# Converting the second chunk of w_out in two halves in a fused FFT and two-layer FFN kernel

## The chip, the cores and the metric

The kernel runs on one core of a Trainium2 chip. The metric is the device time of one execution in microseconds (us). The engines are PE (matrix multiplies, with its weight loads shown apart as PEld), DVE (vector), ACT (scalar), POOL (GpSimd) and SP, which here only issues DMAs. Each engine works through its own instructions in the order in which the program gives them.

## The reference, cut to what matters

```
X = fft(fft(x, axis=1), axis=2).real        # x: 2 x 3008 x 256
h = X @ w_in;  g = where(h > 0, h, exp(min(h, 0)) - 1)
y = g @ w_out                               # w_in 256 x 2048, w_out 2048 x 256
h2 = y @ w2_in; out = (max(h2, 0) + alpha * min(h2, 0)) @ w2_out
```

x and alpha are float32. The four weight matrices come as 64-bit numbers. The kernel has to make 32-bit floats of them itself, on the chip, before it can multiply with them.

## The kernel before, in words

**Stages.** The program builds the Fourier transform out of matrix products (stage_a, a store to DRAM and a load in another order, stage_b), folds the last transform into w_in (w_fold), and runs the first layer as 96 "ticks". A tick t takes one slice f of 128 hidden units over one block of tokens. The first eight ticks are block 0 with f = 0 to 7, the next eight block 1 with f = 0 to 7. The second layer comes after the ticks, in 48 "pairs".

**A tick** (lines 593 to 647) issues, in this order: the "pre" hooks; gemm1(t) on PE (six matmuls, L472); on DVE one pt (L605) and two ht (L609) out of the two PSUM banks; on ACT split_hi of tick t-2 (L584); the "mid" hooks; on ACT Relu (L625) and Exp (L631) of tick t; on POOL split_lo of tick t-2 (two subtractions, L590); on DVE combine of tick t-1 (L577); the "end" hooks; and last on PE gemm2 of tick t-3 (twelve matmuls, L488). Where a tick is the eighth of its block, gemm2 and the copies of its banks (evac, L506 and L508) come earlier in the tick. gemm2 of slice f multiplies with rows 128 f to 128 f + 127 of w_out: slices 0 to 3 need chunk 0, slices 4 to 7 chunk 1. So the first half of chunk 1 is first needed at the end of tick 7, its second half at the end of tick 9, and the second half of chunk 0 at the end of tick 5. Each multiplication is done in three passes with a high and a low part of each operand, and for those slices the second matmul already needs the low part of the weight.

**Converting a chunk.** A chunk of a weight matrix is loaded raw (line 320, an int32 tile of 128 x 4 x 512 for w_out, 8 KB in each partition). conv_y (line 333, ACT) and three steps of conv_s (lines 351, 353 and 355, DVE) make a float32 copy w32 of 128 x 1024 out of it; the steps 0 and 1 work inside the raw tile, and step 2 is the last to read it. Then w_split makes the high part (line 430, ACT) and the low part (line 431, POOL) of one half of 512 columns, in a tile wo of 128 x 2 x 4 x 256, also 8 KB: the high parts are in its first 4 KB, the low parts in its last 4 KB, each with the first half ahead of the second. An argument i restricts conv_y and conv_s to one half of the columns: half i is the raw tile's 4 KB from 4 KB x i on.

**Where the tiles lie.** The pool wp has one buffer for each tag. The raw tile of chunk 1 and its wo tile have the same tag, wo1, so they lie in the same 8 KB. The raw tile of chunk 0 is an exception (line 216): it lies in the buffer of wo3, into which chunk 3 is loaded at the start of tick 4 (line 828). The first w_split of a chunk (i = 0) takes the new tile out of the pool (line 413); no engine waits by hand, the waits come from the order in which tiles are used.

**What sets the order around the change.** Lists written out by hand at the top of the program say in which tick each piece is done. START is the order ahead of tick 0; CONV1 gives the ticks of conv_y, of the three steps and of the two splits of a chunk; FOLD says in which tick w_fold of a chunk of w_in runs (chunk 2: at the start of tick 11, right behind a stage_a). Hooks of one tick and place run in the order in which they were entered. conv_y is a "mid" hook, the steps and the splits are "end" hooks, so a step stands on DVE behind combine of its tick, and a split on ACT behind Exp of its tick.

Of the kernel before, what the change touches and what calls it, by code (L numbers as in the profile page):

```python
# [43 lines left out]
E_PSUM = 42  # L44


CONV1 = [
    (('o', 1, 1), 3, (4, 5, 6), (6, 7)),
    (('i', 1, 2), 7, (7, 8, 9), ()),
    (('i', 1, 3), 10, (10, 12, 13), ()),  # L50
    (('o', 1, 2), 14, (14, 15, 16), (17, 18)),
    (('o', 1, 3), 18, (18, 20, 21), (21, 22)),
# [47 lines left out]
def tile_fft_moe_elu_moe_prelu(  # L100
# [664 lines left out]
    def at(t, fn, *a, where="pre"):  # L765
        hooks[where].setdefault(t, []).append(lambda: fn(*a))
# [4 lines left out]
    def at_conv(t, ts, kind, layer, c, i=None):  # L771

        at(t, conv_y, kind, layer, c, i, where="mid")
        for step in range(3):
            at(ts[step], conv_s, kind, layer, c, i, step, where="end")

    def at_split(t, kind, layer, c, i):
        at(t, w_split, kind, layer, c, i, where="end")
# [7 lines left out]
    with tc.manual_schedule():  # L786
# [27 lines left out]
        }  # L814
        for what, *args in START:
            start[what](*args)
        at_conv(1, (1, 3, 3), "o", 1, 0, 1)
        at_split(3, "o", 1, 0, 1)
        for key, t, ts, splits in CONV1:
            at_conv(t, ts, *key)  # L820
            for i, t_split in enumerate(splits):
# [159 lines left out]
```

## Time and profile before

| | us |
|---|---|
| median of 3 runs | 962.52 (962.43 to 964.06) |
| the profiled execution, its own time | 963.83 |
| its span, first to last instruction | 961.6 |
| PE busy in the span | 947.0 |
| DVE, ACT, POOL busy | 715.8, 654.4, 622.7 |

The profile is of one execution. Its span leaves out some 2 us around the first and the last instruction. Times below are us from the start of the span. The change lies in ticks 1 to 10, which are in the first 95 us.

### The profile page before, as it was taken

The numbers are of one execution on the slowest core, as the hardware profiler recorded it, in microseconds if no ns is written. First come the engines' busy times: TensorE is split into PE (matmuls) and PEld (weight loads), VectorE is DVE, ScalarE is ACT, GpSimd is POOL, SyncE is SP. The second block draws the span as 40 slices with busy tenths as digits, with TensorE's granted clock in tenths as the row PEclk, the third lists the DMA queues.
The fourth block names the chain that finished last, engine by engine and source line by source line (L and its number), as shares of the span: only waits on it lengthen the run. The fifth ranks groups of instructions, "written<-read, shape, count | busy, mean of one in ns | idle before, by whom it ended". The sixth has DMA issues, their size and how long they took to land.

```text
span 961.6 us, 12199 instructions
## 1 busy us (share of the span) xinstructions
PE 947.0 (98%) x4206; PEld 769.3 (80%) x4206; DVE 715.8 (74%) x1012; ACT 654.4 (68%) x914; POOL 622.7 (65%) x495
## 2 busy tenths in 40 slices
PE   8889999999999999999999999999999999999998
PEld 3666778789888878888888888889988888888886
DVE  2896899988999999887777666565657557566564
ACT  5677777766888888888766665565665556565553
POOL 1264577764968779987878855656565664664543
PEclk9999999999999999999999999999999999999999
DMA  8973322201222311121140110020010011001001
GB/s 325 321 228 79 96 77 89 99 25 65 78 75 81 136 44 34 45 88 44 44 154 1 39 45 0 1 88 1 1 56 28 0 45 44 1 1 45 0 1 44
DMA packets 27189, 64.10 MB, mean 67 GB/s; under 512 B 3124, under 2 KB 11572, under 8 KB 25080
## 3 DMA queue, kind: packets, MB, share of 16 engines
q1 hardware_dynamic: 25696, 62.09, 19.3%
q10 hardware_dynamic: 1176, 1.07, 0.3%
q8 instruction: 33, 0.54, 0.2%
q0 software_dynamic: 256, 0.17, 0.1%
q14 instruction: 28, 0.23, 0.1%
HBM read 41.53 MB, written 21.79 MB: 66 GB/s over the span
## 4 chain that ended last, share of the span: by engine, by line
PE 88%; DVE 5%; DMA 3%; ACT 1%; issue 1%; SPq 0%; POOL 0%; ACTq 0%; DVEq 0%
PE acc L488 50%; PE eet L667 13%; PE mmt L667 10%; PE mmt L472 9%; PE eet L472 2%; DMA w<-w_in 1%; DVE et L577 1%; DVE ht L609 1%; DVE pt L605 1%; PE mmt L182 1%; DMA nd<-dt 1%; PE eet L376 1%; PE mmt L281 1%; DMA xc<-x 1%; PE mmt L280 1%
## 5 line engine op out<-in xcount | busy, mean ns | idle before, releaser
L488 PE MATMUL acc<-hi,wo 128*128 128x512 f32 (+1 forms) x1536 | 430.5, 387 | 4.2 <-ACT wo L430 1.5
L693 POOL TENSOR_TENSOR lo<-et,hi 128x512 fp32r<-128x512 f32 (+1 forms) x190 | 237.6, 1281 | 181.0 <-ACT hi L687 181.0
L590 POOL TENSOR_TENSOR lo<-et,hi 128x512 fp32r<-128x512 f32 (+1 forms) x192 | 272.1, 1440 | 107.2 <-ACT hi L584 61.1
L488 PEld LDWEIGHTS acc<-hi,wo 128*128 128x128 f32 x1536 | 288.7, 188 | 61.1 <-ACT wo L430 2.0
L488 PE MATMUL acc<-lo,wo 128*128 128x512 f32 (+1 forms) x768 | 258.3, 387 | 1.3 <-POOL lo L590 1.1
L687 ACT ACTIVATE hi<-et 128x1024 fp32r<-128x1024 f32 (+1 forms) x96 | 100.3, 1045 | 132.5 <-PE acc L488 70.2
L488 PEld LDWEIGHTS acc<-lo,wo 128*128 128x128 f32 x768 | 144.1, 188 | 30.6 <-POOL lo L590 3.4
L625 ACT ACTIVATE et<-ht 128x1024 f32<-128x1024 f32 (+2 forms) x97 | 100.3, 1034 | 68.4 <-DVE ht L609 67.2
L719 DVE TENSOR_TENSOR v<-mmt,p 128x512 f32<-128x512 f32 (+1 forms) x48 | 32.7, 681 | 143.0 <-ACT p L714 143.0
L472 PE MATMUL mmt<-zt,wi 128*128 128x512 f32 (+1 forms) x444 | 116.5, 394 | 1.4 <-DVE ht L609 0.8
L584 ACT ACTIVATE hi<-et 128x1024 fp32r<-128x1024 f32 (+2 forms) x97 | 99.3, 1024 | 5.4 <-DVE et L577 3.9
L609 DVE TENSOR_TENSOR ht<-pt,mmt 128x512 f32<-128x512 f32 (+1 forms) x150 | 95.0, 674 | 8.4 <-PE acc L488 0.5
L472 PEld LDWEIGHTS mmt<-zt,wi 128*128 128x128 f32 x444 | 82.5, 188 | 23.1 <-DVE ht L609 3.4
L744 ACT ACTIVATE et<-mmt 128x512 f32<-128x512 f32 (+1 forms) x96 | 55.8, 590 | 28.8 <-PE mmt L667 14.7
L605 DVE SCALAR_TENSOR_TENSOR pt<-zb,an_sb,mmt 128x512 f32<-128x512 f32 (+1 forms) x73 | 53.4, 731 | 24.7 <-PE mmt L472 24.6
L577 DVE SCALAR_TENSOR_TENSOR et<-et,ht 128x1024 f32<-128x1024 f32 (+2 forms) x44 | 67.3, 1530 | 1.3 <-POOL lo L590 1.1
L574 DVE SCALAR_TENSOR_TENSOR et<-eet,ht 128x512 f32<-128x512 f32 (+1 forms) x106 | 67.1, 674 | 0.0
L747 DVE SCALAR_TENSOR_TENSOR et<-et,oma_sb,eet 128x512 f32<-128x512 f32 (+1 forms) x96 | 66.1, 730 | 0.0
L747 DVE SCALAR_TENSOR_TENSOR et<-et,oma_sb,mmt 128x512 f32<-128x512 f32 (+1 forms) x96 | 66.0, 728 | 0.0
L636 ACT ACTIVATE eet<-et 128x512 f32<-128x512 f32 (+1 forms) x106 | 58.9, 588 | 3.7 <-DVE et L574 2.1
L667 PE MATMUL eet<-xo,wi 128*128 128x512 f32 (+1 forms) x216 | 59.8, 385 | 0.0
L667 PE MATMUL mmt<-xo,wi 128*128 128x512 f32 (+1 forms) x216 | 59.8, 385 | 0.0
(123 smaller groups left out, 1241.6 us busy)
## 6 DMA issues: line engine op xcount, KB each, us to landing
w<-w_in SPq DMA_DIRECT2D x8, 1024.0 KB, 13.5
w<-w_out SPq DMA_DIRECT2D x7, 1024.0 KB, 8.9
ud<-uc SPq DMA_DIRECT2D x20, 256.0 KB, 4.1
vt<-ud SPq DMA_DIRECT2D x5, 1024.0 KB, 4.8
xd<-xs SPq DMA_DIRECT2D x10, 512.0 KB, 3.5
xs<-xd SPq DMA_DIRECT2D x5, 1024.0 KB, 4.8
out_t<-ot SPq DMA_DIRECT2D x16, 256.0 KB, 2.1
xc<-x SPq DMA_DIRECT2D x5, 768.0 KB
```

The costliest lines, as they stand in the source:

```text
L472: mm(out=p[:, 0:n], lhsT=lhsT, rhs=rhs, start=(i == 0), stop=(i == len(ops) - 1))
L488: mm(out=accs[L, bl][d][t][:, 0:n], lhsT=w[:, a, o, d * 128:(d + 1) * 128], rhs=(hi, lo)[b][:, t, 0:n], start=(f == first and i == 0), sto ...
L574: stt(out=s["e"][:, i, :], in0=s["x"][i], scalar=-1.0, in1=s["h"][:, i, :], op0=ALU.add, op1=ALU.max)
L577: stt(out=s["e"][:, i], in0=s["e"][:, i], scalar=-1.0, in1=s["h"][:, i], op0=ALU.add, op1=ALU.max)
L584: act(out=s["hi"][:, i, 0:s["n"]], in_=s["e"][:, i], func=ACTF.Copy)
L590: nc.gpsimd.tensor_tensor(out=s["lo"][:, i, 0:n], in0=s["e"][:, i, :], in1=s["hi"][:, i, 0:n].bitcast(F32), op=ALU.subtract)
L609: tt(out=ht[:, i, 0:n], in0=pt[:, 0:n], in1=p[1], op=op)
L625: act(out=s["e"][:, i], in_=s["h"][:, i], func=ACTF.Relu, scale=-1.0)
L667: mm(out=bank[:, 0:n], lhsT=w[:, a], rhs=x2[b][:, 0:n], start=(first and m == 0), stop=(last and m == 2), skip_group_check=True)
L687: act(out=s["hi"][f][:, :, 0:n], in_=s["g"][f], func=ACTF.Copy)
L693: eng.tensor_tensor(out=s["lo"][f][:, t, 0:n], in0=s["g"][f][:, t], in1=s["hi"][f][:, t, 0:n].bitcast(F32), op=ALU.subtract)
L747: stt(out=o, in0=o, scalar=oma_sb[:, 2 * j + f:2 * j + f + 1], in1=h, op0=ALU.mult, op1=ALU.add)
```

## The change

The second half of chunk 0, which was in at_conv and at_split by hand, and chunk 1 move into a list of halves. For the second half of chunk 0, step 2 and the split go from the end of tick 3 to the end of tick 4. Chunk 1 was converted as a whole (conv_y in tick 3, the steps at the ends of ticks 4, 5 and 6, the splits at the ends of ticks 6 and 7). Now its first half has conv_y in tick 3, the steps at the ends of ticks 4, 5 and 5, and the split at the end of tick 6; its second half has conv_y in tick 5, the steps at the ends of ticks 6, 7 and 7, and the split at the end of tick 8. Chunk 2 of w_in goes one tick later: conv_y from tick 7 to 8, the steps from the ends of ticks 7, 8 and 9 to those of 8, 9 and 10. In tick 6 the first half's split is entered ahead of the second half's step 0.

```diff
+HALVES = [
+    (('o', 1, 0), 1, 1, (1, 3, 4), 4),
+    (('o', 1, 1), 0, 3, (4, 5, 5), 6),
+    (('o', 1, 1), 1, 5, (6, 7, 7), 8),
+]
 CONV1 = [
-    (('o', 1, 1), 3, (4, 5, 6), (6, 7)),
-    (('i', 1, 2), 7, (7, 8, 9), ()),
+    (('i', 1, 2), 8, (8, 9, 10), ()),
     (('i', 1, 3), 10, (10, 12, 13), ()),
...
             start[what](*args)
-        at_conv(1, (1, 3, 3), "o", 1, 0, 1)
-        at_split(3, "o", 1, 0, 1)
+        for key, i, t, ts, t_split in HALVES:
+            at_conv(t, ts, *key, i)
+            at_split(t_split, *key, i)
         for key, t, ts, splits in CONV1:
```

## Rows read from the trace of the kernel before

**Rows 1.** The page's busy times, and its chain that ended last, by engine.
```profile
PE 947.0 (98%) x4206; PEld 769.3 (80%) x4206; DVE 715.8 (74%) x1012; ACT 654.4 (68%) x914; POOL 622.7 (65%) x495
...
PE 88%; DVE 5%; DMA 3%; ACT 1%; issue 1%; SPq 0%; POOL 0%; ACTq 0%; DVEq 0%
```

**Rows 2.** Busy time by stretch: PE, PEld, DVE, ACT, POOL, PE's granted clock, DMA.
```profile
70.00:72.00 2.00, 2.00 (x6) 1.53 (x5) 1.51 (x2) 1.97 (x3) 2.00 (x2) 0.50 0.00 0
...
74.00:76.00 2.00, 2.00 (x7) 1.11 (x7) 0.00 (x0) 1.27 (x3) 0.65 (x1) 1.00 0.00 0
```

**Rows 3.** PE's instructions in order of time: start, us, line, count, [idle before].
```profile
39.12 2.14 PE L488 MATMUL acc<-hi,wo 128*128 128x512 f32 x8 [1.47 <-ACT hi L584]
...
55.42 1.98 PE L488 MATMUL acc<-hi,wo 128*128 128x512 f32 x8
...
64.35 1.95 PE L472 MATMUL mmt<-zt,wi 128*128 128x512 f32 x6
67.84 0.49 PE L488 MATMUL acc<-hi,wo 128*128 128x512 f32 x1 [1.53 <-ACT wo L430]
69.20 3.21 PE L488 MATMUL acc<-hi,wo 128*128 128x512 f32 x7 [0.87 <-POOL wo L431]
...
82.32 1.98 PE L488 MATMUL acc<-hi,wo 128*128 128x512 f32 x8
...
90.83 3.60 PE L376 MATMUL eet<-w,c_sb 128*128 128x512 f32 x8
```

**Rows 4.** The chain that ended last, in order of time.
```profile
69.20 4.37 PE acc L488 x11
...
76.65 2.72 PE acc L488 x12
```

**Rows 5.** DVE's instructions in order of time.
```profile
31.52 0.43 DVE L351 TENSOR_SCALAR w<-w 128x512 int32<-128x512 int32 x1
...
33.17 0.68 DVE L353 SCALAR_TENSOR_TENSOR w<-w 128x512 int32<-128x512 int32 x1
...
54.23 1.79 DVE L351 TENSOR_SCALAR w<-w 128x1024 int32<-128x1024 int32 x1
...
62.16 0.73 DVE L605 SCALAR_TENSOR_TENSOR pt<-zb,an_sb,mmt 128x512 f32<-128x512 f32 x1
...
65.91 1.21 DVE L355 SCALAR_TENSOR_TENSOR w<-w,w 128x1024 int32<-128x1024 int32 x1
67.04 0.73 DVE L605 SCALAR_TENSOR_TENSOR pt<-zb,an_sb,mmt 128x512 f32<-128x512 f32 x1
...
69.08 1.22 DVE L577 SCALAR_TENSOR_TENSOR et<-et,ht 128x1024 f32<-128x1024 f32 x1
...
76.01 0.75 DVE L605 SCALAR_TENSOR_TENSOR pt<-zb,an_sb,mmt 128x512 f32<-128x512 f32 x1 [4.00 <-PE mmt L472]
...
85.10 2.31 DVE L355 SCALAR_TENSOR_TENSOR w<-w,w 128x1024 int32<-128x1024 int32 x1
...
91.71 0.70 DVE L351 TENSOR_SCALAR w<-w 128x1024 int32<-128x1024 int32 x1
```

**Rows 6.** ACT's instructions in order of time.
```profile
54.36 1.06 ACT L631 ACTIVATE et<-et 128x1024 f32<-128x1024 f32 x1
...
65.47 1.06 ACT L631 ACTIVATE et<-et 128x1024 f32<-128x1024 f32 x1
67.16 0.63 ACT L430 ACTIVATE wo<-w 128x512 fp32r<-128x512 f32 x1 [0.62 <-DVE w L355]
...
79.33 1.06 ACT L631 ACTIVATE et<-et 128x1024 f32<-128x1024 f32 x1
```

**Rows 7.** POOL's instructions in order of time.
```profile
67.86 1.28 POOL L431 TENSOR_TENSOR wo<-w,wo 128x512 fp32r<-128x512 f32 x1 [2.96 <-ACT wo L430]
...
87.31 2.54 POOL L590 TENSOR_TENSOR lo<-et,hi 128x512 fp32r<-128x512 f32 x2 [0.98 <-PE acc L488]
```

**Rows 8.** SP's DMA issues in order of time.
```profile
58.71 0.41 SPq L320 DMA_DIRECT2D w<-w_out  x1
```

## The prediction, made before the changed kernel was run

> **What bounds the kernel now.** The page comes first: PE is busy for 947.0 of 961.6 us, and 88% of the chain that ended last is PE's [rows 1]. So a wait of PE that the change adds or removes goes into the time in full, and work of other engines counts only where PE waits for it. For such waits I read PE's instructions in order of time. In the stretch that the change touches there is one place that matters, gemm2 of tick 4, the first user of chunk 1: PE is idle for 1.53 us until ACT has the high part of the first half, does one matmul, and is idle for 0.87 us more until POOL has the low part [rows 3]. By then the granted clock has fallen: it is 0.50 from 70 to 72 us, PE's lower level of 1.2 GHz, after those two idle stretches, and 1.00 again from 74 [rows 2]. The chain gives the price: the last eleven matmuls take 4.37 us there, where twelve take 2.72 a tick later, so eleven at full clock are worth 2.5 [rows 4] and the low clock costs 1.9.
>
> What does this split wait for? DVE's last step on the whole chunk runs from 65.91 to 67.12 [rows 5], ACT's split starts at 67.16, POOL's at 67.86 and ends at 69.14 [rows 6, 7], PE goes on at 69.20. After that PE leads: DVE is idle for 4.00 us until gemm1 of tick 8 [rows 5].
>
> **Release of the first half.** The change converts the first half early, but enters its split in tick 6 while the raw words of the second half are still at work. Split and raw words share one buffer. The first half's low part has bytes 4096 to 6143 of each partition; the raw second half has 4096 to 8191, and its step 2 comes at the end of tick 7. So the low part cannot be written before that step is done, if the output is still to be right. Waits for a buffer are kept for a tile as a whole, I take it, so the high part on ACT waits too.
>
> On DVE that step 2 stands behind the pt, the two ht and the combine of tick 7. Before, these ran behind the last step on the chunk, from 67.04 to 69.08 + 1.22 = 70.30 [rows 5]: 3.3 us that now lie ahead of the release. The steps change as well. Before: 1.79 (slowed by POOL) and twice 1.21, 4.2 us [rows 5]. After: twice 0.43 + 0.68 + 0.68, 3.6 us [rows 5], 0.6 less; if one is slowed as the 1.79 was (1.1 over the 0.70 of the same step elsewhere [rows 5]), 0.5 more. The release is later by 2.7 to 3.8 us; I take **3.2**, the middle, near 70.3. ACT's 0.63 and POOL's 1.28 follow as before, so PE goes on at 72.4 instead of 69.20. Its eleven matmuls then cost 4.37 again, since the idle time ahead of them is longer than the one after which the clock fell. If the high part need not wait, 0.7 less. The clock may be kept or stay low for longer: 1.9 to either side.
>
> While ACT is held, Relu and Exp of tick 7, split_hi of tick 5 and the copies of stage_a wait behind the split, and POOL's pair for tick 5 waits for that split_hi. Their users are in tick 8, behind gemm2 of tick 4 on PE, which is itself held for as long; ACT's 3.2 us of backlog fits, as DVE's 4.00 us of idle time there shows [rows 5]. Cost 0.
>
> A rule speaks for a higher price. DVE's step over 1024 columns takes 1.21 us in one place and 2.31 where POOL runs its pair [rows 5]. The Trainium skill (SBUF — State Buffer, "Who interferes with whom") says that a DVE instruction with two SBUF inputs and a GpSimd one that reads SBUF exclude each other, and the later one waits the other out. By that rule two half steps at the end of tick 7 could each wait for a POOL subtraction, 1.28 us, and the release would be up to 2.6 later. I don't take this: POOL's pair of tick 5 is itself behind the held split, so nothing runs on POOL then.
>
> **w_in's chunk 2 a tick later.** Its last step moves to the end of tick 10, behind the combine, where before step 0 of chunk 3 started, at 91.71 [rows 5]. With 1.21 us [rows 5] it ends at 92.92. PE starts w_fold on this chunk at 90.83 [rows 3], first in tick 11 but for a stage_a, with no idle time now. It must wait for the whole copy: **2.1 us**. POOL's pair of that tick ends at 87.31 + 2.54 = 89.85 [rows 7], so the step isn't slowed; were it, 2.31, the wait would be 3.2. If DVE gets to tick 10 1.1 us earlier, because the step of tick 9 is quick (1.21 instead of 2.31 [rows 5]), it is 1.0. An idle 1.47 us ahead of 39.12 left eight matmuls at 2.14 us, full clock [rows 3], so I take no clock loss; the bound is 1.9 again. What stands behind the waiting matmuls is all of PE's work, so nothing hides it.
>
> **What costs nothing.** Chunk 0's second half: its split goes behind Exp of tick 4, which ended at 55.42 [rows 6]; with 0.63 and 1.28 its low part is there by 57.4, so the second matmul of gemm2 at 55.42 [rows 3] waits for up to 1.7 us, eleven more end by 59.9 and the first three of gemm1 in tick 6 by 60.6. DVE came to that tick's pt at 62.16 [rows 5], so it stays the later of the two; without this cover up to 1.7. Chunk 1's second half: Exp of tick 8 ends at 80.39 [rows 6], plus 0.63 and 1.28 is 82.3; PE's second matmul there is due at 82.32 + 0.23 [rows 3, 4]. Just in time; up to 1.1 if POOL is slowed. conv_y of w_in's chunk 2 goes on ACT from tick 7 into tick 8, where ACT waits for DVE, as it does in most ticks. The moved steps issue no DMA; the one DMA that waits for them, chunk 3 into the buffer of raw chunk 0, was issued at 58.71 [rows 8], and step 2 on chunk 0 will be done by about 55.
>
> **The sum.** 3.2 + 2.1 = +5.3 us. On the profiled execution's own 963.83 that is 969.1; that run lies 1.3 above the median of 962.52, so for a median I say 962.5 + 5.3 = **967.8**. Since PE is the bound to the end [rows 1], nothing gives it back.
>
> **Rivals.** About 0.2%, 1.9 us, is what a measurement of this kernel can tell from no change.
> - *The early split works.* If the first half is not held (the change then does what it seems to say), ACT splits behind Exp of tick 6, which ended at 66.53 [rows 6], POOL ends 1.9 us later at 68.4, PE's eleven matmuls take 2.5 and end at 70.9 instead of 73.6: -2.7. With the wait of w_fold, -0.6, 961.9, no change. For it: DVE's work on the first half is done well ahead. Against it: the shared buffer.
> - *It works and w_fold hardly waits.* The faster side: -2.7 with a wait of 0 to 1.0 at 90.83, 959.8 to 960.8. It decides if DVE's last step on w_in's chunk 2 ends less than 0.8 us after PE is ready for it. Against it: DVE has the combine of tick 9 ahead of that step.
> - *Held, but w_fold doesn't wait:* +3.2, 965.7. This needs DVE 2.1 us ahead in tick 10, and it was slowed by POOL in tick 9.
> - *The clock falls at w_fold too:* an idle 2.1 us costs 1.9 more, +7.2, 969.7. Against it, the 1.47 us that cost none; for it, that 1.53 and 0.87 together did.
> - *The change hardly does what it says:* chunk 0's second half and chunk 1's early steps matter to nobody; that is part of my forecast, since their covers hold.
>
> **How the numbers follow.** Forecast 0.73, clock at w_fold 0.09, held without a wait at w_fold 0.06, early split with the wait 0.08, early split without 0.04. The first three are slower: 0.88; then 0.08 the same and 0.04 faster. The range holds the first three with their bounds: 967.8 - 1.9 (clock kept at gemm2) - 1.1 (w_fold's shorter wait) = 964.8, and 967.8 + 1.9 + 0.6 (the release's upper bound) = 970.3. About 0.83 lies in it; the cases at 959.8 to 961.9 stay out.
>
> **What will show it.** ACT's first L430 on chunk 1 should wait for DVE's L355 of 512 columns and start near 70.3, not near 66.5, with PE's idle time ahead of gemm2 of tick 4 grown from 2.4 to 5.6 us or so. PE should wait near 94 us for DVE's L355 of 1024 columns ahead of L376, for about 2 us. If that first split starts before 67, or PE has no wait ahead of w_fold, the forecast is wrong, at that step.

## The result and the profile after

The changed kernel takes 973.79 us in the median of 6 runs (972.75 to 974.55), the kernel before 963.29 beside it. The ratio is 1.0106, with a 95% interval from 1.0093 to 1.012: 10.2 us slower. The profiled execution took 974.1 us with a span of 972.0, which is 10.3 and 10.4 over the one shown before. So the way was forecast, and the size was half of what came: +5.3 was said, and 970.3 at most.

In the changed kernel's lines gemm2 is L492, gemm1 L476, w_fold's matmuls L380, ACT's split L434 and POOL's L435, and the steps of conv_s are L355, L357 and L359. The page's busy times, and its chain by engine, changed kernel (answers to [rows 1]):

```profile
PE 950.8 (98%) x4206; PEld 770.5 (79%) x4206; DVE 717.2 (74%) x1015; ACT 654.5 (67%) x915; POOL 624.0 (64%) x495
...
PE 87%; DVE 8%; issue 2%; ACT 1%; DMA 1%; POOL 0%; SPq 0%; ACTq 0%; DVEq 0%
```

DVE has 1.4 us more to do and PE 3.8, the latter at the low clock. What grew besides is waiting: PE is idle for 21.2 us of the span, where it was idle for 14.6. PE's instructions in order of time, changed kernel (answers to [rows 3]):

```profile
56.52 0.50 PE L492 MATMUL acc<-hi,wo 128*128 128x512 f32 x1 [0.62 <-ACT wo L434]
57.88 1.88 PE L492 MATMUL acc<-hi,wo 128*128 128x512 f32 x7 [0.85 <-POOL wo L435]
...
65.91 1.95 PE L476 MATMUL mmt<-zt,wi 128*128 128x512 f32 x6
73.06 0.80 PE L492 MATMUL acc<-hi,wo 128*128 128x512 f32 x1 [5.19 <-ACT wo L434]
74.41 3.35 PE L492 MATMUL acc<-hi,wo 128*128 128x512 f32 x7 [0.55 <-POOL wo L435]
...
80.81 1.93 PE L476 MATMUL mmt<-zt,wi 128*128 128x512 f32 x6
...
99.24 5.40 PE L380 MATMUL eet<-w,c_sb 128*128 128x512 f32 x8 [2.12 <-DVE w L359]
104.07 1.95 PE L476 MATMUL mmt<-zt,wi 128*128 128x512 f32 x6
```

Both forecast waits are there. PE waits 5.19 and 0.55 us ahead of gemm2 of tick 4, where it waited 1.53 and 0.87 [rows 3], and 2.12 us ahead of w_fold, where it did not wait. A third, ahead of gemm2 of tick 2 (0.62 and 0.85), is the one that the prediction held to be covered. The eleven matmuls behind the first wait, in the chain that ended last (answers to [rows 4]), and the first two places in the busy times by stretch (PE, PEld, DVE, ACT, POOL, PE's granted clock, DMA; answers to [rows 2]):

```profile
74.41 5.06 PE acc L492 x11
```

```profile
70.00:72.00 2.00, 0.00 (x0) 0.00 (x0) 1.97 (x3) 0.00 (x0) 0.00 (x0) 1.00 0.00 0
...
74.00:76.00 2.00, 1.59 (x4) 1.31 (x5) 0.00 (x0) 1.97 (x3) 1.31 (x2) 0.50 0.00 0
...
100.00:102.00 2.00, 2.00 (x4) 0.77 (x3) 0.00 (x0) 0.00 (x0) 0.00 (x0) 0.55 0.60 122
```

From 70 to 72 us DVE is the only engine at work: PE, ACT and POOL all stand behind it. After each of the two forecast waits PE runs at its lower level (0.50 and 0.55). Why DVE comes so late is in its own row, and ACT and POOL show what waits for what (answers to [rows 5, 6, 7]):

```profile
54.03 1.78 DVE L359 SCALAR_TENSOR_TENSOR w<-w,w 128x512 int32<-128x512 int32 x1
55.73 0.41 DVE L355 TENSOR_SCALAR w<-w 128x512 int32<-128x512 int32 x1
...
60.83 1.78 DVE L357 SCALAR_TENSOR_TENSOR w<-w 128x512 int32<-128x512 int32 x1
62.65 1.66 DVE L359 SCALAR_TENSOR_TENSOR w<-w,w 128x512 int32<-128x512 int32 x1
...
67.41 0.42 DVE L355 TENSOR_SCALAR w<-w 128x512 int32<-128x512 int32 x1
...
70.93 0.69 DVE L357 SCALAR_TENSOR_TENSOR w<-w 128x512 int32<-128x512 int32 x1
71.65 0.69 DVE L359 SCALAR_TENSOR_TENSOR w<-w,w 128x512 int32<-128x512 int32 x1
```

```profile
67.55 1.06 ACT L635 ACTIVATE et<-et 128x1024 f32<-128x1024 f32 x1
72.38 0.63 ACT L434 ACTIVATE wo<-w 128x512 fp32r<-128x512 f32 x1 [3.77 <-DVE w L359]
```

```profile
51.75 3.50 POOL L594 TENSOR_TENSOR lo<-et,hi 128x512 fp32r<-128x512 f32 x2 [1.58 <-issue]
...
58.52 6.93 POOL L594 TENSOR_TENSOR lo<-et,hi 128x512 fp32r<-128x512 f32 x4 [0.69 <-POOL wo L435]
```

The first half was ready at 64.31 (62.65 + 1.66). Its split started at 72.38, 0.04 us after the second half's last step (71.65 + 0.69 = 72.34). And three half steps that ran beside POOL's pairs, from 51.75 and from 58.52 on, took 1.78, 1.78 and 1.66 us, where the same steps on the same size take 0.69 at 70.93 and 71.65.

Where the 10.4 us of span came from, by the starts of the same work in the two traces. Up to gemm2 of tick 1 the changed trace is 0.3 us later; it is so at 24 us already, ahead of every moved piece, so this has nothing to do with the change. The release (72.34 against 67.12) is later by 5.2, of which 4.9 is the change. The twelve matmuls and the stage_a behind them lose 0.9 more at the low clock, so that gemm1 of tick 8 starts 6.1 later (80.81 against 74.72). The wait ahead of w_fold adds 2.3 (99.24 against 90.83 is 8.4) and its low clock 1.8 (gemm1 of tick 11 starts 4.8 us after w_fold, at 104.07, where it was 3.0 before). That makes 10.2; the last 0.2 are spread over the rest of the trace.

### The profile page after: what moved, and what is told of

It reads as the page before. It is cut to its first block, busy times and chain, and to the rows that moved or that the text cites. A ratio compares the mean times of both kernels' runs of the same rounds, so it can differ in the third digit from the quotient of the medians.

```text
span 972.0 us, 12203 instructions
## 1 busy us (share of the span) xinstructions
PE 950.8 (98%) x4206; PEld 770.5 (79%) x4206; DVE 717.2 (74%) x1015; ACT 654.5 (67%) x915; POOL 624.0 (64%) x495
## 4 chain that ended last, share of the span: by engine, by line
PE 87%; DVE 8%; issue 2%; ACT 1%; DMA 1%; POOL 0%; SPq 0%; ACTq 0%; DVEq 0%
PE acc L492 48%; PE eet L671 13%; PE mmt L671 10%; PE mmt L476 9%; PE eet L476 2%; DVE et L581 2%; DVE ht L613 2%; DVE pt L609 1%; DVE w L357 1%; PE mmt L186 1%; PE eet L186 1%; DVE w L359 1%; PE eet L380 1%; DMA xc<-x 1%; PE mmt L285 1%
## 5 line engine op out<-in xcount | busy, mean ns | idle before, releaser
L492 PE MATMUL acc<-hi,wo 128*128 128x512 f32 (+1 forms) x1536 | 431.4, 388 | 9.1 <-ACT wo L434 5.8
L492 PEld LDWEIGHTS acc<-hi,wo 128*128 128x128 f32 x1536 | 288.9, 188 | 66.9 <-ACT wo L434 6.7
L492 PE MATMUL acc<-lo,wo 128*128 128x512 f32 (+1 forms) x768 | 258.9, 388 | 1.3 <-POOL lo L594 1.1
L492 PEld LDWEIGHTS acc<-lo,wo 128*128 128x128 f32 x768 | 144.3, 188 | 30.7 <-POOL lo L594 3.4
L476 PE MATMUL mmt<-zt,wi 128*128 128x512 f32 (+1 forms) x444 | 116.5, 394 | 0.9 <-DVE ht L613 0.8
L476 PEld LDWEIGHTS mmt<-zt,wi 128*128 128x128 f32 x444 | 82.6, 188 | 22.3 <-DVE ht L613 3.2
```

The source lines that it names most:

```text
L476: mm(out=p[:, 0:n], lhsT=lhsT, rhs=rhs, start=(i == 0), stop=(i == len(ops) - 1))
L492: mm(out=accs[L, bl][d][t][:, 0:n], lhsT=w[:, a, o, d * 128:(d + 1) * 128], rhs=(hi, lo)[b][:, t, 0:n], start=(f == first and i == 0), sto ...
```

## The experiments

The medians of the kernel before moved between 962.7 and 964.1 from one group of runs to another, so ratios are compared; one per mille is 1 us.

**Chunk 2 of w_in back at its ticks, all else changed.**

```diff
-    (('i', 1, 2), 8, (8, 9, 10), ()),
+    (('i', 1, 2), 7, (7, 8, 9), ()),
```

> The changed kernel with chunk 2 of w_in back at its old ticks (7; 7, 8, 9). My reading of the two traces: the 2.1 us that PE waits ahead of w_fold and the 2.0 us that w_fold then loses at the low clock both go, so this is 4.2 us under the changed kernel, about +6.2 us over the one before, and w_fold takes 3.4 us with no wait ahead of it. Rival: DVE is behind in tick 10 anyway after the long hold, w_fold waits all the same, and the time stays within 1 us of the changed kernel.

Ratio 1.0075 (1.006 to 1.009), +7.2 us. PE's row of this kernel:

```profile
97.23 3.60 PE L380 MATMUL eet<-w,c_sb 128*128 128x512 f32 x8
```

w_fold has no wait and no low clock; the profiled span is 968.1, 3.9 under the changed kernel's. So the wait at w_fold and its low clock cost 3 to 4 us. The rival, that DVE is late in tick 10 whatever is done there, falls.

**Only chunk 2 of w_in a tick later, all else as before.**

```diff
-    (('i', 1, 2), 7, (7, 8, 9), ()),
+    (('i', 1, 2), 8, (8, 9, 10), ()),
```

> The kernel before with only chunk 2 of w_in a tick later. If the wait at w_fold is a matter of DVE's place in tick 10 alone: +4.2 us (2.1 to 2.3 of waiting, 1.9 of low clock). If it needs the hold in tick 7 to put DVE and PE out of step: within 1 us of the kernel before. If the low clock came only because PE had been idle in tick 7 as well: +2.2.

Ratio 1.0044 (1.0029 to 1.0059), +4.2 us. PE's row at w_fold, and the busy time by stretch behind it, of this kernel:

```profile
93.37 5.40 PE L376 MATMUL eet<-w,c_sb 128*128 128x512 f32 x8 [1.99 <-DVE w L355]
```

```profile
94.00:96.00 2.00, 2.00 (x4) 0.77 (x3) 0.00 (x0) 0.02 (x1) 0.00 (x0) 0.54 0.55 110
```

The 2 us wait and the low clock (5.40 us for 3.6) come without any hold in tick 7. The moved step alone is enough.

**The raw words of chunk 1 in another buffer, all else changed.** They go into the buffer of tag sc, whose load of x is put off to tick 8.

```diff
-    ('load', 'i', 1, 2), ('load', 'x', 1, 1), ('load', 'o', 1, 2), ('load', 'x', 1, 2), ('load', 'i', 1, 3),
+    ('load', 'i', 1, 2), ('load', 'x', 1, 1), ('load', 'o', 1, 2), ('load', 'i', 1, 3),
...
-LOAD_X = {3: 9}
+LOAD_X = {2: 8, 3: 9}
...
-        home, tag = (big, "big") if (kind, layer, c) in wd else (wp, f"w{kind}{c}")
+        home, tag = (big, "big") if (kind, layer, c) in wd else (wp, "sc" if (kind, layer, c) == ("o", 1, 1) else f"w{kind}{c}")
```

> The changed kernel with the raw words of chunk 1 in another buffer (that of tag sc, whose load of x moves to tick 8). If the shared buffer holds the first split: ACT's first split on chunk 1 starts right behind Exp of tick 6, near 68.6 instead of 72.4, PE goes on near 70.6 instead of 74.4, and the time is 3.8 to 4.7 us under the changed kernel, +6 to +7 over the one before. If something else holds it (the order of ACT's queue, DVE): no change, +10.5.

Ratio 1.0054 (1.0038 to 1.0071), +5.2 us, 5 under the changed kernel. ACT's and PE's rows of this kernel:

```profile
67.61 1.06 ACT L635 ACTIVATE et<-et 128x1024 f32<-128x1024 f32 x1
68.57 0.61 ACT L434 ACTIVATE wo<-w 128x512 fp32r<-128x512 f32 x1
```

```profile
69.23 0.51 PE L492 MATMUL acc<-hi,wo 128*128 128x512 f32 x1 [1.30 <-ACT wo L434]
70.58 1.89 PE L492 MATMUL acc<-hi,wo 128*128 128x512 f32 x7 [0.84 <-POOL wo L435]
...
74.53 1.95 PE L476 MATMUL mmt<-zt,wi 128*128 128x512 f32 x6
...
92.98 5.40 PE L380 MATMUL eet<-w,c_sb 128*128 128x512 f32 x8 [2.14 <-DVE w L359]
```

The split stands right behind Exp of tick 6, and nothing else in ACT's queue held it: the shared buffer did. Its high part lies in bytes that no raw word of the second half has, and in the changed kernel it waited all the same, so the wait is for the tile as a whole. In this profile, of the fastest of four executions (967.7 to 969.4 us), gemm1 of tick 8 starts 6.3 us earlier than in the changed kernel: 3.8 by the release (70.58 for 74.41), which is what was expected, and 2.4 because the clock stays up behind the shorter wait (seven matmuls in 1.89 us).

**The control: the kernel before with that other buffer and that later load.**

> The kernel before with the same other buffer and the same later load of x: the control for the run before. Both theories: within 0.5 us of the kernel before. If the later load of x costs by itself, more, and the run before has to be read against this one.

Ratio 1.0007 (0.9998 to 1.0017). The other buffer costs nothing that can be told, so the 5 us above are the hold's.

**POOL without its reads for the activations of ticks 2 to 4, all else changed.** POOL writes zeros in place of the low parts of those activations, which it makes in ticks 4 to 6; they are left out of the products.

```diff
         for i in range(2):
+            if t in (2, 3, 4):
+                nc.gpsimd.memset(s["lo"][:, i, 0:n].bitcast(F32), 0.0)
+                continue
```

> The changed kernel, where POOL writes zeros for the low parts of the activations of ticks 2, 3 and 4 in place of its subtractions, so those low parts are left out. If POOL's reads are what made DVE's half steps slow (1.78, 1.78 and 1.66 us for 0.69): they take about 0.7, the last step on chunk 1 ends 3 to 4 us earlier, near 68.8 instead of 72.3, and the time is 3 to 4.5 us under the changed kernel. If half steps are slow by themselves, in those places: no change, +10.5 over the kernel before.

Ratio 1.0091 (1.0074 to 1.0108), +8.8 us: 1.4 under the changed kernel, less than expected, and the two intervals overlap, so that the 1.4 rests on the rows below. DVE's and POOL's rows of this kernel, where the steps keep the lines L357 and L359 and pt is L612:

```profile
53.86 0.69 DVE L359 SCALAR_TENSOR_TENSOR w<-w,w 128x512 int32<-128x512 int32 x1
...
59.69 0.69 DVE L357 SCALAR_TENSOR_TENSOR w<-w 128x512 int32<-128x512 int32 x1
60.41 0.69 DVE L359 SCALAR_TENSOR_TENSOR w<-w,w 128x512 int32<-128x512 int32 x1
...
66.32 0.75 DVE L612 SCALAR_TENSOR_TENSOR pt<-zb,an_sb,mmt 128x512 f32<-128x512 f32 x1 [1.69 <-PE mmt L476]
...
70.23 0.69 DVE L359 SCALAR_TENSOR_TENSOR w<-w,w 128x512 int32<-128x512 int32 x1
```

```profile
59.90 1.00 POOL L595 MEMSET lo<- 128x512 f32 x2 [2.04 <-PE acc L492]
```

All three steps fall to 0.69 us. Beside the one at 53.86 POOL does nothing, and beside the two from 59.69 on it writes zeros: so POOL's reads were what made them slow, and its writes do not. But of the 3.2 us that DVE gains on the three steps, more than half goes into idle time, 1.69 us of it ahead of pt of tick 7, where DVE now waits for PE's gemm1. The last step ends at 70.92, 1.4 earlier than in the changed kernel. That is what POOL's reads cost on the path.

**Only chunk 0's second half a tick later, all else as before.**

```diff
-        at_conv(1, (1, 3, 3), "o", 1, 0, 1)
-        at_split(3, "o", 1, 0, 1)
+        at_conv(1, (1, 3, 4), "o", 1, 0, 1)
+        at_split(4, "o", 1, 0, 1)
```

> The kernel before with only the first part of the change: step 2 and the split of chunk 0's second half at the end of tick 4. My prediction's cover: PE waits in gemm2 of tick 2, DVE is later in any case, 0 to +0.5 us. Rival: the step now meets POOL's pair (1.78 us for 0.69), DVE's row without a gap is lengthened by 1.1 us, which goes into the release of chunk 1 in full: about +1.1. Cover gone altogether: +1.7.

Ratio 1.0003 (0.9994 to 1.0013): nothing. PE's and POOL's rows of this kernel:

```profile
57.28 0.49 PE L488 MATMUL acc<-hi,wo 128*128 128x512 f32 x1 [1.09 <-ACT wo L430]
58.63 3.08 PE L488 MATMUL acc<-hi,wo 128*128 128x512 f32 x7 [0.86 <-POOL wo L431]
...
70.07 2.40 PE L488 MATMUL acc<-hi,wo 128*128 128x512 f32 x8
```

```profile
69.24 1.30 POOL L431 TENSOR_TENSOR wo<-w,wo 128x512 fp32r<-128x512 f32 x1 [2.96 <-ACT wo L430]
```

PE now waits ahead of gemm2 of tick 2, and hardly ahead of gemm2 of tick 4: it arrives there at 70.07, when the high part is done, and loses some 0.4 us (2.40 for eight matmuls that take 1.98 elsewhere), since POOL ends the low part at 70.54 (69.24 + 1.30). One wait took the other's place, the low clock with it. The step did meet POOL (1.78 us), as its rival said, but of the later release PE feels only these 0.4 us.

**Both costs undone: the other buffer, and chunk 2 of w_in at its old ticks.** The edits are those of the first and third experiment together.

> The changed kernel with both costs undone: the raw words of chunk 1 in the buffer of tag sc, and chunk 2 of w_in at its old ticks. If the hold by the shared buffer and the wait of w_fold are the whole of the loss, what is left is the halves themselves: PE's wait ahead of gemm2 of tick 4 ends near 70.6, 1.1 us later than before with the shift of the trace, and the time is 0 to +1.5 us over the kernel before. Rival, a cost of the halves that neither run has shown (DVE's extra instructions, POOL's reads): +3 us or more.

Ratio 1.0015 (1.0006 to 1.0024), +1.4 us: inside what was expected. The hold and w_fold are 8.8 of the 10.2 us; undone one at a time they gave 5 and 3. PE's row of this kernel:

```profile
70.56 1.86 PE L492 MATMUL acc<-hi,wo 128*128 128x512 f32 x7 [0.86 <-POOL wo L435]
```

PE goes on at 70.56 where it was 69.20 [rows 3], 1.4 later, which fits what is left. The split now stands behind Exp of tick 6, and that is late because DVE reaches the tick's pt later, behind its slowed steps. That this is the whole of the rest is argued, not shown by a run.

**The early split that the halves allow.** The run before, with the first half split at the end of tick 5, where its last step stands, and chunk 0's second half back at tick 3.

```diff
-    (('o', 1, 0), 1, 1, (1, 3, 4), 4),
-    (('o', 1, 1), 0, 3, (4, 5, 5), 6),
+    (('o', 1, 0), 1, 1, (1, 3, 3), 3),
+    (('o', 1, 1), 0, 3, (4, 5, 5), 5),
```

> The run before, with the first half's split at the end of tick 5 and chunk 0's second half back at tick 3: halves as they could have been meant. The split starts near 62 instead of 68.6, PE has no wait ahead of gemm2 of tick 4, and the time is 2.5 to 4.5 us under the kernel before. If what PE waits for there only moves on to the low part of tick 4's activation, which POOL then makes behind the split, or to DVE in tick 8: within 1.5 us of the kernel before.

Ratio 0.9997 (0.9988 to 1.0006): no gain. PE's row of this kernel:

```profile
65.91 1.98 PE L492 MATMUL acc<-hi,wo 128*128 128x512 f32 x8
...
79.07 0.51 PE L492 MATMUL acc<-hi,wo 128*128 128x512 f32 x1 [1.11 <-ACT wo L434]
80.42 2.97 PE L492 MATMUL acc<-hi,wo 128*128 128x512 f32 x7 [0.85 <-POOL wo L435]
```

The wait ahead of gemm2 of tick 4 is gone. A new one of nearly the same size (1.11 and 0.85 us for 1.53 and 0.87), with the low clock behind it, stands ahead of gemm2 of tick 6, the first user of the second half, whose split at the end of tick 8 was in time in the changed kernel only because PE was late. Neither the low part of the activation nor DVE in tick 8, which the expectation named, took the gain back.

**The second half's split a tick earlier too.**

```diff
-    (('o', 1, 1), 1, 5, (6, 7, 7), 8),
+    (('o', 1, 1), 1, 5, (6, 7, 7), 7),
```

> The run with the first half's split in tick 5, with the second half's split at the end of tick 7 instead of 8. That run removed PE's wait ahead of gemm2 of tick 4 and showed a new one of 1.1 and 0.85 us ahead of gemm2 of tick 6, behind the second half's split, with the low clock after it. If that new wait is all that took the gain back: no wait there, and the time is 2.5 to 4 us under the kernel before, level with the run that converts the whole chunk a tick earlier or up to 1 us better. If DVE, which reaches the second half's last step near 73.6, holds ACT in tick 7 and the wait moves to another tick: within 1 us of the kernel before.

Ratio 0.9968 (0.9956 to 0.9981), 3.1 us faster than before. PE's row of this kernel shows both places without a wait for the split:

```profile
65.81 1.98 PE L492 MATMUL acc<-hi,wo 128*128 128x512 f32 x8
...
77.92 1.98 PE L492 MATMUL acc<-hi,wo 128*128 128x512 f32 x8
```

**No halves: the whole chunk done a tick earlier.** One line of the kernel before.

```diff
-    (('o', 1, 1), 3, (4, 5, 6), (6, 7)),
+    (('o', 1, 1), 3, (4, 5, 5), (5, 6)),
```

> The kernel before with chunk 1 as a whole, but its last two steps both at the end of tick 5 and its splits at the ends of ticks 5 and 6: no halves, no other buffer. If the place of the split behind DVE's steps is all that PE waited for: ACT's split starts near 63.5 instead of 67.2, PE hardly waits ahead of gemm2 of tick 4, and the time is 2 to 4 us under the kernel before. If DVE is the bound in these ticks (no gap from 49 to 72): pt of tick 6 comes 1.2 to 2.3 us later, gemm1 and the stages behind it wait, and the time is within 1 us of the kernel before.

Ratio 0.9971 (0.996 to 0.9983), 2.8 us faster than before and 13 faster than the changed kernel. ACT's and PE's rows of this kernel:

```profile
64.28 0.63 ACT L430 ACTIVATE wo<-w 128x512 fp32r<-128x512 f32 x1 [3.23 <-DVE w L355]
```

```profile
67.16 2.01 PE L488 MATMUL acc<-hi,wo 128*128 128x512 f32 x8
```

ACT is held for 3.23 us, and that costs nothing, since PE is at gemm2 of tick 4 only at 67.16. The two faster kernels differ by less than their intervals; this one needs no halves and no other buffer.

**The kernel before once more.**

> The kernel before once more, for a look at how its low clock falls from one execution to the next: either 69.2 us and eleven matmuls at 4.37 us as in the profile shown, or full clock and 2.5, with a time 1.5 to 2 us lower.

962.94 us. PE's row and the stretch behind it:

```profile
68.43 0.49 PE L488 MATMUL acc<-hi,wo 128*128 128x512 f32 x1 [1.57 <-ACT wo L430]
69.79 1.88 PE L488 MATMUL acc<-hi,wo 128*128 128x512 f32 x7 [0.87 <-POOL wo L431]
...
73.73 1.95 PE L472 MATMUL mmt<-zt,wi 128*128 128x512 f32 x6
```

```profile
70.00:72.00 2.00, 2.00 (x10) 1.63 (x10) 1.54 (x2) 2.00 (x3) 1.58 (x1) 1.00 0.00 0
```

The same two idle stretches as in [rows 3], and this time the clock stays at 1.00. From 69.79 to gemm1 of tick 8 it is 3.9 us, where the profile shown before has 5.5: the low clock is worth 1.6. The time is 0.9 lower, not 1.5 to 2, since this execution comes to that place 0.6 us later. The 58 executions of the kernel before that ran beside the experiments fit this price: the 33 with a mean granted clock of 0.998 to 1.000 have a median of 962.6 us, the 25 with 0.996 or 0.997 one of 964.1. All executions of the two faster kernels have 0.998 or more: a part of what they gain is that PE's wait is gone, and the fall of the clock with it.

## Why the prediction was wrong in its size

**The hold: right.** The first half's split waited for the second half's last step, by the buffer that they share, high part and all. The other buffer took the hold away, and its control shows that this buffer has no gain or cost of its own.

**The release, 3.2 us said and 4.9 found: mis-sized.** The step that failed is the sentence "After: twice 0.43 + 0.68 + 0.68, 3.6 us", with an allowance for one slowed step. In the trace the six half steps take 0.41 + 1.78 + 1.66 + 0.42 + 0.69 + 0.69 = 5.65 us, 1.5 over the middle of what was said, and chunk 0's moved step, which the sum had at no cost, 1.78, 1.1 over its time in the kernel before:

```profile
50.44 0.69 DVE L355 SCALAR_TENSOR_TENSOR w<-w,w 128x512 int32<-128x512 int32 x1
```

DVE's combines in ticks 4 to 6 gave 0.7 back (4.24 us in all for 4.92), and the last 0.2 is the overlap of neighbouring rows. POOL's pairs lie beside the ends of ticks 4 and 5, and that is where the change put the early steps. The Trainium skill (SBUF — State Buffer, "Who interferes with whom") says that a DVE instruction with two SBUF inputs contends with a GpSimd instruction that reads SBUF, and not with one that only writes it. The traces agree on both counts: 1.66 to 1.78 beside POOL's subtractions, 0.69 beside its writes of zeros. The prediction used that rule for the end of tick 7 alone and turned it down there, rightly, as 0.69 twice shows; it was needed two and three ticks earlier. With POOL's reads gone the last step ended at 70.92, near the 70.3 that was said. So taking them away gives back 1.4 of the 1.7 us that were missing; more it could not give, since DVE then waits for PE.

**The low clock behind it: 0.9 us short.** It was taken as 4.37 for eleven matmuls, as before. It was 5.06, and went on into stage_a. It lay within the bound of 1.9. Why it stayed low for longer is open.

**The wait of w_fold: right,** 2.1 said, 2.3 by the traces, and PE waited 2.0 in the kernel with this part alone.

**The low clock at w_fold: the second failed step.** "An idle 1.47 us ahead of 39.12 left eight matmuls at 2.14 us, full clock, so I take no clock loss." It cost 1.8 us. That case was a rival with a chance of 0.09. The row chosen for it was of a shorter wait; the nearer one, with 2.4 us of idle time in two pieces and the low clock behind it, was in the same rows. And the chosen row does not hold for every execution. The same wait in the same place, in the kernel with the first half's split in tick 5:

```profile
39.16 3.17 PE L492 MATMUL acc<-hi,wo 128*128 128x512 f32 x8 [1.47 <-ACT hi L588]
```

There the granted clock was 0.50 from 40 to 43 us and the eight matmuls took 3.17 us; in the other twelve profiles they took 2.10 to 2.14.

**The covers: right for PE.** In the changed kernel PE waits 0.62 and 0.85 us ahead of gemm2 of tick 2, and DVE comes to the next pt without a pause, as was said. Chunk 0's later split, taken alone, costs nothing, though by another way than was said: PE's wait there takes the place of the one in tick 4. What was not covered is the moved step itself on DVE, the 1.1 us above.

**The range.** It was built from one unknown at a time. The misses, 1.7, 0.9, 0.2 and 1.8, all fell on the same side, and the two largest were outside what it held: it took 0.6 for a later release, and the clock at one of the two waits only. Even the rival with the low clock at w_fold came to 969.7. The 1.8 does not hang on the others: it came in the kernel with that part alone.

## What to carry to other kernels

A piece converted early is not available early if its place is still taken: look up whose bytes the first write goes to, and who reads them last. When a step is moved, look up what the engine whose reads slow such a step (here POOL) does at the new place, and take each of the moved steps at that price; and give a wait of PE of some 2 us, besides its length, the price of the low clock that came behind it each time at w_fold here (1.8 us). If a consumer waits for the last link of a chain, try first to move that link (here one line, 2.8 us) before cutting the work into pieces; and after a gain look for the next user of the same chain, since it may have been just in time only because the first was late.

## What the runs showed of the hardware

- POOL's reads made half steps of DVE take 1.66 to 1.78 us for 0.69; POOL's writes did not lengthen them. POOL's pair was lengthened too, from 2.54 [rows 7] to 3.50. The step with one input was slowed as well: 0.42 alone, 1.53 beside a pair in the kernel with the split in tick 5:

```profile
54.27 1.53 DVE L355 TENSOR_SCALAR w<-w 128x512 int32<-128x512 int32 x1
```

- The clock after a wait of PE is not the same from one execution to the next: after idle stretches of 1.57 and 0.87 us it was 1.00 in one profile of the kernel before, and after 1.53 and 0.87 it was 0.50 in another. After 1.47 it stayed up in twelve profiles and fell in one. After the wait of about 2 us at w_fold (1.99 to 2.14) it was low in all four profiles that have it (5.40 us for 3.6 each time).
